# Another order of the first 100 steps of an attention and mixture-of-experts kernel on one Trainium2 core

## The chip, the core and the metric

The kernel runs as one program on one core of a Trainium2 chip. Five engines work side by side, each through its own queue in order: PE (TensorE, matrix products), DVE (VectorE), ACT (ScalarE), POOL (GpSimd) and SP (SyncE, which here issues nearly all transfers). Sixteen DMA engines move the data. The metric is the device time of one execution in microseconds (us); lower is better.

## The reference

Three parts follow each other. First, attention in which a query sees only the keys of its own bucket (a bucket is the sign pattern of six projections):

```python
q_bits = (np.einsum('bhsd,dk->bhsk', q, proj) > 0)
k_bits = (np.einsum('bhsd,dk->bhsk', k, proj) > 0)
mask = q_bucket[:, :, :, None] == k_bucket[:, :, None, :]
scores = np.where(mask, scale * np.matmul(q, k.transpose(0, 1, 3, 2)), -1e9)
attn = softmax(scores)
x = np.matmul(attn, v)
...
h = x @ w_in
x = (h * (1.0 / (1.0 + np.exp(-1.702 * h)))) @ w_out
...
logits = x @ w_gate + np.log1p(np.exp(x @ w_noise)) * noise
...
out[mask] += top2_w[mask, k, None] * (np.maximum(x[mask] @ w1[e], 0.0) @ w2[e])
```

Shapes: 2 batches, 8 heads, 768 positions, head width 64; so 1536 tokens of width 512. The feed-forward is 512 to 2048 to 512. The last part sends each token to 2 of 8 experts (512 to 1024 to 512). The weights `w_in` and `w_out` arrive as 64-bit numbers.

## The kernel before, in words

**Steps.** The attention is cut into 96 steps (`NU`), one for each batch, third of the positions, head and 128 queries. Six chunks of 16 steps make up the tokens: chunk 0 is steps 0 to 15, and so on. A loop over `g` emits for each step the scores of step g+2 (`qk`, line 250), the row maximum of step g+1 (`rowmax`, line 262, DVE), its exponential (`expo`, line 271, ACT), and the turning of the weights of step g. For steps 0 to 15 that turning is a transpose on PE (`e_turn`, line 289) and a copy out of PSUM (`e_copy`, line 297 or 299). From step 16 on it is a high half (`e_hi`, line 310, ACT), a low half (`e_lo`, lines 317 and 319) and a transposing DMA (line 323, `et<-er`). The buffers `er` of this last path are two, and they share their tag with the value blocks `v32` of the first chunk.

**Around it.** Everything else hangs on step numbers in a table `PARAM`. `KA` and `QA` say at which step a block of keys or queries is loaded (two steps ahead), split into halves (`stack_hi`, `stack_lo`), turned by DMA (line 169), projected (`buckets`, lines 186 and 187), compared (`one_hot`, line 197) and turned a second time with its bits (`stack_end`, line 205). `VA` does this for the values (lines 224, 225 and 232), `PV` for the products with the values (`pv`, lines 357 and 364) whose result is scaled and split into `xt` (`pv_scale` line 373, `pv_norm` line 380, `pv_out` lines 389 to 395). `ST` sets at which step a chunk's feed-forward begins, `RA` and `R1` when its routing runs, `O0` when the output is zeroed.

**Weight blocks.** The feed-forward weights come in 32 blocks of 512 KB: 0 to 15 of `w_in`, 16 to 31 of `w_out`. `W` gives each its step. A block is loaded (`w_load`, line 414, three buffers `wraw`), its 64-bit numbers are made 32-bit ones by three DVE operations (`w_bits`, lines 424, 427, 430), it is scaled (line 443 on POOL or 445 on ACT, by the table `WS`), its high half taken (line 446, ACT) and its low half (line 447, POOL). Only then is the buffer free for the block three later.

**Feed-forward.** `moe_pe` gives 16 pieces a chunk: eight of the first product (line 467, tiles `h`) and eight of the second (line 478, tiles `px`). Behind each `h` come a tanh (line 485, ACT), a product (line 497, DVE), a high half (line 511, ACT) and a low half (line 513, POOL or DVE by the table `GS`).

**What sets the order.** Up to step 99 the code only states in which order instructions are emitted; a scheduler then orders every engine's queue. From step 100 (`GM=100`) the order is the one written. So a number in the table does not fix a place; it changes what the scheduler sees, and the queues below show what came of it. On the chip each queue then runs strictly as it stands.

After the steps come the experts: products at lines 843, 868 and 874, each expert's weights split at lines 782 and 783, all in written order.

Of the kernel before, what the change touches and what calls it, by code (L numbers as in the profile page):

```python
# [57 lines left out]
PARAM = dict(GM=16, HE=lambda nm, b: 'D', OE=lambda nm, b: 'D', SC=lambda nm, b: 'D', WB=0, XO=lambda b: 'D', NG=16, WS=lambda i: 'P', TS=lambda g: True, XL=lambda g: 'D', GW=2, E0=7, T0=12, T1=16, EL=8, WX=3, PV={(1,2,3):4}, PVD=5, ST={}, VA={}, RA={}, O0=48, OS=2, IS=2, FU=16, VF=2, EC=lambda g: 'AA', QX=8, QS=3, EA=1, S1=(8,8,8,9,9,9,11,13), QE=8, XG=2, XB=2, PC=2, OH=3, BK=3, R0=18, R1=0, LK=8, WL=1, NW=3, LE=lambda nc: nc.scalar, I0=24, LQ=8, LV=0, W=[(g, 1) for g in range(-6, 30)], KA={(0,0,0):-8,(0,0,1):-6,(0,1,0):-4,(0,1,1):-2}, QA={(0,0,0):-7,(0,0,1):-3}, HI=lambda g: 'P', LO=lambda g: False)  # L58
PARAM.update(KA={(0, 0, 0): -15, (0, 0, 1): -6, (0, 1, 0): -5, (0, 1, 1): -4, (0, 2, 0): -1, (0, 2, 1): 1, (0, 3, 0): 4, (0, 3, 1): 5, (1, 0, 0): 37, (1, 0, 1): 39, (1, 1, 0): 44, (1, 1, 1): 46, (1, 2, 0): 42, (1, 2, 1): 51, (1, 3, 0): 47, (1, 3, 1): 51}, QA={(0, 0, 0): -15, (0, 0, 1): -3, (0, 0, 2): 1, (0, 0, 3): 3, (0, 1, 0): 8, (0, 1, 1): 9, (0, 1, 2): 17, (0, 1, 3): 21, (0, 2, 0): 24, (0, 2, 1): 28, (0, 2, 2): 30, (0, 2, 3): 33, (1, 0, 0): 37, (1, 0, 1): 41, (1, 0, 2): 47, (1, 0, 3): 52, (1, 1, 0): 57, (1, 1, 1): 56, (1, 1, 2): 60, (1, 1, 3): 69, (1, 2, 0): 72, (1, 2, 1): 69, (1, 2, 2): 80, (1, 2, 3): 84}, VA={(0, 0, 0): -1, (0, 0, 1): -3, (0, 1, 0): -1, (0, 1, 1): -1, (0, 2, 0): 0, (0, 2, 1): 0, (0, 3, 0): -1, (0, 3, 1): -2, (1, 0, 0): -1, (1, 0, 1): -1, (1, 1, 0): 2, (1, 1, 1): -4, (1, 2, 0): -3, (1, 2, 1): -3, (1, 3, 0): 2, (1, 3, 1): -2}, PV={(0, 0, 0): 4, (0, 0, 1): 5, (0, 0, 2): 6, (0, 0, 3): 5, (0, 1, 0): 6, (0, 1, 1): 4, (0, 1, 2): 4, (0, 1, 3): 5, (0, 2, 0): 5, (0, 2, 1): 5, (0, 2, 2): 5, (0, 2, 3): 6, (1, 0, 0): 4, (1, 0, 1): 5, (1, 0, 2): 4, (1, 0, 3): 5, (1, 1, 0): 5, (1, 1, 1): 5, (1, 1, 2): 5, (1, 1, 3): 6, (1, 2, 0): 6, (1, 2, 1): 4, (1, 2, 2): 4, (1, 2, 3): 4}, RA={0: 18, 1: 18, 2: 19, 3: 24, 4: 18}, W=[(g,1) for g in [-6, -4, -3, -1, 0, 0, 1, 1, 2, 4, 4, 7, 8, 8, 9, 10, 11, 12, 13, 14, 15, 16, 16, 17, 18, 20, 20, 22, 22, 23, 23, 24]], EC=lambda g:'AA', LE=lambda nc:nc.sync, HI=lambda g:'AAAA'[g%4], LO=lambda g:[0, 0, 0, 1, 0, 0, 0, 1][g%8]==1, S1=[8, 8, 8, 8, 8, 11, 13, 22], ST={0: 4, 1: 4, 2: 5, 3: 4, 4: 5, 5: 3}, NG=28, WS=lambda i:'PAAA'[i%4], HE=lambda nm,b:'DPDD'[2*(nm=='k')+b], OE=lambda nm,b:'DTDD'[2*(nm=='k')+b], SC=lambda nm,b:'DADD'[2*(nm=='k')+b], R1=2, I0=26, IS=1, O0=56, OS=1, GM=100, BK=3, OH=3, QX=7, QS=3, QE=8, VF=0, T0=12, T1=17, EL=10, WX=5, WL=2, PC=2, GW=2, E0=8, WB=2)

PARAM.update(H0=((15,1),(16,3)),H1=((0,5),(2,1)),HG=((1,1),),RT=0,E1=16,SL=1,QS=3)
# [1183 lines left out]
```

## Time and profile before

| what | value |
|---|---|
| time, median of 3 runs | 804.14 us (797.45 to 805.53) |
| the profiled execution's own time | 802.09 us |
| its span on the core | 800.3 us |
| what lies around the span | 1.8 us |
| PE busy | 705.8 us, 88% |
| DVE busy | 502.0 us, 63% |
| ACT busy | 457.7 us, 57% |
| POOL busy | 269.2 us, 34% |
| mean granted TensorE clock | 0.961 of full speed |

Busy shares are means over stages that have different limits. The steps run until about 450 us: row maximum 0 starts at 23.26 us, number 9 at 57.46, number 15 at 90.75, number 20 at 108.71, number 32 at 170.40, number 72 at 356.27 and number 95 at 450.66. The experts fill the last 250 us. The clock and the engines' shares are best read stage by stage between these marks.

### The profile page before, as it was taken

How to read it: one execution, taken by the hardware profiler on the slowest of the kernel's cores; microseconds unless marked ns; L12 is line 12 of the kernel's file. 1: busy time of each engine (PE TensorE's matmuls, PEld its weight loads, DVE VectorE, ACT ScalarE, POOL GpSimd, SP SyncE). 2: the span in 40 equal slices, each digit the busy share in tenths (PEclk: the TensorE clock that was granted, in tenths of full speed). 3: DMA queues.
4: the chain of work that ended last, by engine and by line, in shares of the span. 5: the costliest groups of instructions: out<-in, count | busy, mean ns of one | idle time of the engine just before them, and what ended most of it. 6: DMA issues, size and time to landing. Idle time of an engine off the chain costs nothing.

```text
span 800.3 us, 14889 instructions
## 1 busy us (share of the span) xinstructions
PE 705.8 (88%) x5408; PEld 434.1 (54%) x5409; DVE 502.0 (63%) x1251; ACT 457.7 (57%) x974; POOL 269.2 (34%) x338
## 2 busy tenths in 40 slices
PE   1776778988988889889989999998999999999995
PEld 0544446546744665467457667556555545555452
DVE  7986889887875788568667716672835427344220
ACT  4789877777776787467668514443543535435220
POOL 7445546552453355025122123241030211302113
PEclk9976889999989999999999999999999999999998
DMA  8999589999999999985696590658958568483213
GB/s 222 239 278 252 158 198 190 286 249 207 180 209 169 173 196 208 190 169 105 102 190 121 100 283 8 175 190 246 261 80 264 145 164 250 62 264 84 27 17 44
DMA packets 266941, 139.19 MB, mean 174 GB/s; under 512 B 224176, under 2 KB 242672, under 8 KB 266864
## 3 DMA queue, kind: packets, MB, share of 16 engines
q1 hardware_dynamic: 260848, 125.04, 67.3%
q0 software_dynamic: 6016, 13.16, 9.3%
q8 instruction: 43, 0.70, 0.4%
q14 instruction: 34, 0.28, 0.1%
HBM read 61.48 MB, written 23.20 MB: 106 GB/s over the span
## 4 chain that ended last, share of the span: by engine, by line
PE 39%; DMA 4%; DVE 3%; ACT 2%; issue 1%; POOL 1%; POOLq 0%; ACTq 0%; DVEq 0%
PE ph L843 15%; PE py L874 14%; PE px L478 5%; PE h L467 3%; DMA et<-er 3%; PE py L868 2%; PE pv L364 1%; DMA xg<-slots 1%; ACT er L310 1%; DMA slots<-xr,si 1%; PE s L250 0%; DVE er L319 0%; DVE th L497 0%; ACT ew L782 0%; POOL out_dram L891 0%
## 5 line engine op out<-in xcount | busy, mean ns | idle before, releaser
L467 PE MATMUL h<-xt,wi 128*128 128x256 f16 x1152 | 140.4, 278 | 11.6 <-ACT xt L393 5.6
L843 PE MATMUL ph<-xg,ew 128*128 128x400 f16 (+2 forms) x864 | 134.2, 317 | 3.6 <-DMA xg<-slots 2.9
L478 PE MATMUL px<-wo,gt 128*128 128x512 f16 x576 | 131.0, 380 | 0.4 <-DVE th L497 0.4
L467 PEld LDWEIGHTS <-wi 128*128 128x128 f16 x1152 | 113.1, 100 | 33.4 <-issue 13.4
L783 DVE SCALAR_TENSOR_TENSOR ew<-w,ew 128x1024 f16<-128x1024 f32 x64 | 77.8, 1226 | 82.3 <-ACT ew L782 82.3
L874 PE MATMUL py<-ew,ht 128*128 128x512 f16 x576 | 126.0, 379 | 0.0
L250 PE MATMUL s<-kt,qt 128*128 128x512 f16 (+3 forms) x384 | 89.9, 356 | 37.1 <-DVE e L262 26.2
L891 POOL DMA_INDIRECT out_dram<-yo,ti x32 | 49.9, 1558 | 207.2 <-ACT yo L884 196.4
L843 PEld LDWEIGHTS <-ew 128*128 128x128 f16 x864 | 81.9, 100 | 53.6 <-issue 5.6
L319 DVE SCALAR_TENSOR_TENSOR er<-e,mx,er 128x768 f16<-128x768 f32 x68 | 71.5, 1055 | 42.0 <-ACT er L310 40.8
L262 DVE TENSOR_SCALAR_CACHE_REDUCE e<-s 128x768 f32<-128x768 f32 x96 | 90.7, 949 | 4.4 <-PE s L250 1.4
L874 PEld LDWEIGHTS <-ht 128*128 128x128 f16 x576 | 56.3, 98 | 66.8 <-issue 0.2
L271 ACT ACTIVATE e<-e,mx 128x768 f32<-128x768 f32 x96 | 89.3, 930 | 1.7
L478 PEld LDWEIGHTS <-gt 128*128 128x128 f16 x576 | 55.0, 98 | 63.9 <-issue 2.0
L513 POOL TENSOR_TENSOR gt<-th,gt 128x512 f16<-128x512 f32 x48 | 56.5, 1176 | 97.8 <-ACT gt L511 94.7
L310 ACT ACTIVATE er<-e,mx 128x768 f16<-128x768 f32 x68 | 62.9, 930 | 33.2 <-DMA et<-er 31.1
L250 PEld LDWEIGHTS <-qt 76*128 76x128 f16 (+1 forms) x384 | 35.5, 102 | 67.4 <-issue 31.3
L884 ACT ACTIVATE yo<-py,wv 128x512 f32<-128x512 f32 x24 | 16.5, 687 | 93.4 <-PE py L874 56.7
L853 ACT ACTIVATE ht<-ph 128x400 f16<-128x400 f32 (+2 forms) x72 | 33.5, 465 | 57.5 <-PE ph L843 57.3
L782 ACT ACTIVATE ew<-w 128x1024 f16<-128x1024 f32 x64 | 66.2, 1048 | 0.1
L364 PE MATMUL pv<-et,vt 128*64 128x256 f16 x720 | 51.3, 285 | 11.4 <-DMA et<-er 11.3
L854 DVE SCALAR_TENSOR_TENSOR ht<-ph,ht 128x400 f16<-128x400 f32 (+2 forms) x72 | 37.4, 524 | 35.9 <-ACT ht L853 35.6
(230 smaller groups left out, 914.3 us busy)
## 6 DMA issues: line engine op xcount, KB each, us to landing
w<-in_moe_w_dram SPq DMA_DIRECT2D x64, 512.0 KB, 5.5
wraw<-in_moe_w_in_dram SPq DMA_DIRECT2D x16, 512.0 KB, 5.7
wraw<-in_moe_w_out_dram SPq DMA_DIRECT2D x16, 512.0 KB, 5.0
slots<-blank SPq DMA_DIRECT2D x6, 1032.0 KB, 7.4
v<-in_v_dram SPq DMA_DIRECT2D x24, 192.0 KB, 3.7
out_dram<-zeros SPq DMA_DIRECT2D x13, 256.0 KB
k<-in_k_dram SPq DMA_DIRECT2D x16, 192.0 KB, 4.0
q<-in_q_dram SPq DMA_DIRECT2D x24, 128.0 KB, 3.7
```

The source lines that it names most:

```text
L250: nc.tensor.matmul(ps[:, n0 * 128:n1 * 128], qt[:kr, s, h, t, :], kt[:kr, s, h, n0:n1, :].rearrange("p c t -> p (c t)"), start=(s == 0), s ...
L262: nc.vector.tensor_scalar(e32, st[g]["ps"][:, :S], -FAR, -TOP, op0=OP.max, op1=OP.max, accum_out=mx[:, 0:1])
L271: nc.scalar.activation(e32, e32, AF.Exp, scale=0.125, bias=st[g]["mx"][:, 1:2], accum_out=sms[b, cc, hp][:, 2 * h + t:2 * h + t + 1] if g ...
L310: nc.scalar.activation(er[:, 0], st[g]["e"], AF.Copy, scale=r)
L319: nc.vector.scalar_tensor_tensor(er[:, 1], d["e"], d["mx"][:, 3:4], er[:, 0], op0=OP.mult, op1=OP.subtract)
L364: nc.tensor.matmul(po[h * 64:h * 64 + 64, 0, :], vt[:, c, vs, h * 64:h * 64 + 64], et[h][:, es * NT + c].rearrange("p t q -> p (t q)"), st ...
L467: nc.tensor.matmul(ph[:, a, :], wi[ws][:, d, f0:f0 + 128], xt[:, d, xs, :], start=(d == 0 and ws == 0 and xs == 0), stop=(d == HP - 1 and ...
L478: nc.tensor.matmul(px, gts[ci, f // 2][:, gs, f % 2, t * 128:t * 128 + 128], wo[ws][:, f, :], start=(f == 0 and gs == 0 and ws == 0), stop ...
L782: nc.scalar.activation(hi, x, AF.Copy, scale=SW1 if j == 0 else SW2)
L783: nc.vector.scalar_tensor_tensor(lo, x, SW1 if j == 0 else SW2, hi, op0=OP.mult, op1=OP.subtract)
L843: nc.tensor.matmul(ph[:, :c1 - c0], w[:, ws, d * FE + f * 128:d * FE + f * 128 + 128], xg[e, p][:, xs * HP + d, :], start=(d == 0 and ws = ...
L874: nc.tensor.matmul(py, ht[:, f, hs, t * 128:t * 128 + 128], w[:, ws, f * DM:(f + 1) * DM], start=(i == 0), stop=(i == n - 1))
```

## The change

One line is added that replaces numbers and letters of the table; no function changes. All line numbers of the code below it grow by two.

```diff
+PARAM.update(KA={(0, 0, 0): -19, (0, 0, 1): -6, (0, 1, 0): -5, (0, 1, 1): -5,
...
+W=[(g_,1) for g_ in [-6, -4, -3, -1, 0, 0, 1, 1, 2, 3, 6, 6, 7, 8, 9, 10, 10, 10, 11, 12, 12, 12, 15, 15, 19, 20, 21, 23, 23, 26, 28, 29]],
...
+EC=lambda g:2*'AAAAAAADADAAAAAA'[g%16],
...
```

What differs, old value to new:

- Keys and queries: first key block from step -15 to -19, block (0,1,1) from -4 to -5, block (1,0,1) from 39 to 42, two later ones by one step. Query blocks (0,0,2) from 1 to -1, (0,0,3) from 3 to 1, (0,1,0) from 8 to 7, (0,1,3) from 21 to 19, two of batch 1 by one step.
- Values of head pair 0: `VA` -1 to 2 and -3 to -4.
- Value products `PV` (steps behind the unit's start): (0,0,0) 4 to 6, (0,0,1) 5 to 4, (0,0,2) 6 to 5, (0,1,2) 4 to 7, (1,2,2) 4 to 5.
- Weight blocks `W`: before `-6 -4 -3 -1 0 0 1 1 2 4 4 7 8 8 9 10 11 12 13 14 15 16 16 17 18 20 20 22 22 23 23 24`, now the list in the diff.
- `ST`: chunk 1's feed-forward from 4 to 6 steps behind its last attention step. `RA`: routing of chunk 2 from 19 to 22, of chunk 3 from 24 to 26; `R1` 2 to 0, so the last routing piece comes two steps sooner. `O0` 56 to 57.
- Engines: the two copies of line 297 in each of steps 7 and 9 from ACT to DVE; four low halves of line 513 (chunk 0 piece 7, chunk 1 piece 0, chunk 2 pieces 4 and 5) from POOL to DVE; the scaling of weight blocks 0, 12 and 24 from POOL to ACT; the high half of step 25 from ACT to POOL.

Three places show what the scheduler made of it.

The first is SP's queue between weight blocks 11 and 13 (blocks 11 and 12 are `wraw_677` and `wraw_717` before, `wraw_621` and `wraw_663` now; `v32` are value blocks). Before:

```order
L414 DMA wraw_677<-in_moe_w_in_dram 128x1024
L120 DMA q32_735<-in_q_dram 128x2x128
L120 DMA q32_778<-in_q_dram 128x2x128
L215 DMA v32_833<-in_v_dram 128x384 x2
L124 DMA v32_1107<-in_v_dram 128x384
L124 DMA v32_1196<-in_v_dram 128x384
L124 DMA v32_1290<-in_v_dram 128x384
L124 DMA v32_1292<-in_v_dram 128x384
L414 DMA wraw_717<-in_moe_w_in_dram 128x1024
```

Now:

```order
L416 DMA wraw_621<-in_moe_w_in_dram 128x1024
L207 DMA_TRANSPOSE qt_509<-qsb_458 128x4x128
L122 DMA q32_782<-in_q_dram 128x2x128
L416 DMA wraw_663<-in_moe_w_in_dram 128x1024
L171 DMA_TRANSPOSE qt_828<-qsa_787 128x4x128
L217 DMA v32_850<-in_v_dram 128x384 x2
L126 DMA v32_1014<-in_v_dram 128x384
L122 DMA q32_1185<-in_q_dram 128x2x128
L207 DMA_TRANSPOSE kt_659<-ks_638 128x6x128
L416 DMA wraw_694<-in_moe_w_in_dram 128x1024
```

Eight loads of queries and values stood between blocks 11 and 12; one load and a transpose stand there now, and the value loads are spread behind block 12.

The second is ACT's queue where the last quarter of chunk 0's `xt` is made, just before the first feed-forward (`er` are the high halves of steps 17 and 18, `xn` is `pv_scale`, `xt` is `pv_out`). Before:

```order
L310 ACTIVATE er_1186<-e32_1182 128x768
L310 ACTIVATE er_1218<-e32_1214 128x768
L373 ACTIVATE xn_1275<-pv_1232 128x256
L446 ACTIVATE wo0_92<-wraw_1063 128x512
L393 ACTIVATE xt_732<-xn_1275 128x256
```

Now:

```order
L312 ACTIVATE er_1210<-e32_1206 128x768
L375 ACTIVATE xn_1280<-pv_1239 128x256
L312 ACTIVATE er_1231<-e32_1227 128x768
L447 ACTIVATE wraw_953<-wraw_953 128x512
L395 ACTIVATE xt_853<-xn_1280 128x256
```

`xn` moved ahead of the second high half. The semaphores moved with it: before, the first `er` waits for a transposing DMA and the second for PE; now the first waits for PE, and the second, behind `xn`, for the DMA.

The third is ACT's queue where chunk 1's feed-forward begins (`th` are its first two tanh tiles, `er` the high halves of steps 35 and 36). Before:

```order
L310 ACTIVATE er_2221<-e32_2215,mx_2214 128x768
L158 ACTIVATE qsa_2275<-q32_2156 128x4x64
L310 ACTIVATE er_2294<-e32_2288,mx_2287 128x768
L485 ACTIVATE th_2411<-h_2379 128x512
L270 ACTIVATE mx_2321<-mx_2321 128x1
L485 ACTIVATE th_2531<-h_2427 128x512
```

Now:

```order
L312 ACTIVATE er_2219<-e32_2213,mx_2212 128x768
L487 ACTIVATE th_2525<-h_2491 128x512
L272 ACTIVATE mx_2321<-mx_2321 128x1
L487 ACTIVATE th_2605<-h_2540 128x512
L312 ACTIVATE er_2294<-e32_2288,mx_2287 128x768
```

The tanh tiles stand between the same exponentials as before, although the table puts the chunk two steps later, and they are now ahead of the second high half.

## Rows read from the trace of the kernel before

**Rows 1.** Page, part 1: busy time and share of each engine.
```profile
PE 705.8 (88%) x5408; PEld 434.1 (54%) x5409; DVE 502.0 (63%) x1251; ACT 457.7 (57%) x974; POOL 269.2 (34%) x338
```

**Rows 2.** Windows: length, then PE, PEld, DVE, ACT, POOL busy; PEclk, DMA share, GB/s.
```profile
23.26:57.46 34.20, 25.52 (x187) 16.47 (x184) 31.04 (x77) 27.47 (x75) 15.58 (x20) 0.87 1.14 259
57.46:92.56 35.10, 25.36 (x166) 15.11 (x165) 25.05 (x56) 30.42 (x80) 20.41 (x26) 0.69 0.91 241
...
108.71:170.40 61.69, 55.88 (x455) 36.84 (x454) 56.14 (x108) 46.49 (x99) 32.79 (x33) 0.93 0.97 229
170.40:356.27 185.87, 163.47 (x1405) 108.09 (x1403) 132.56 (x368) 130.33 (x307) 71.31 (x79) 0.96 1.01 194
...
543.00:800.30 257.30, 247.81 (x1681) 133.86 (x1680) 104.71 (x197) 98.14 (x145) 46.99 (x59) 0.99 0.58 146
```

**Rows 3.** Chain that ended last, in order of time: start, length, what.
```profile
402.72 5.80 DMA et<-er
...
430.26 2.12 PE pv L364 x35
```

**Rows 4.** Timeline at the start: us, length, engine, operation, [idle before <-releaser].
```profile
1.77 0.60 SPq L91 DMA_DIRECT2D p<-in_proj_dram  x1
...
23.26 0.94 DVE L262 TENSOR_SCALAR_CACHE_REDUCE e<-s 128x768 f32<-128x768 f32 x1
23.92 0.22 ACT L191 ACTIVATE pc<-s 128x72 f32<-128x72 f32 x1
```

**Rows 5.** Groups by line and shape: busy us, mean ns of one, idle before.
```profile
L424 DVE TENSOR_SCALAR pfi<-wraw 128x512 int32<-128x512 int32 x32 | 22.1, 690 | 11.7 <-DMA wraw<-in_moe_w_in_dram 10.7 <-DMA wraw<-in_moe_w_out_dram 0.8
L297 ACT ACTIVATE et<-pt 128x384 f32<-128x384 f32 x32 | 15.0, 482 | 1.1 <-PE pt L289 0.9
L380 DVE TENSOR_TENSOR xn<-pv,xn 128x256 f32<-128x256 f32 x7 | 2.9, 413 | 0.0
L513 POOL TENSOR_TENSOR gt<-th,gt 128x512 f16<-128x512 f32 x48 | 56.5, 1176 | 97.8 <-ACT gt L511 94.7 <-PE s L250 2.1 <-issue 0.9
L497 DVE SCALAR_TENSOR_TENSOR th<-th,h 128x512 f32<-128x512 f32 x48 | 32.6, 679 | 14.2 <-ACT th L485 9.6 <-issue 4.5
```

**Rows 6.** Timeline of DVE and POOL around 24 us.
```profile
23.05 0.28 DVE L197 TENSOR_TENSOR ks<-pc 128x36 f16<-128x36 f32 x2
...
23.95 1.15 POOL L447 TENSOR_TENSOR wi<-wraw,wi 128x512 f16<-128x512 f32 x1 [0.93 <-ACT wi L446]
24.17 1.10 DVE L197 TENSOR_TENSOR ks<-pc 128x36 f16<-128x36 f32 x2
```

**Rows 7.** Timelines of SP, DVE and POOL between 54 and 75 us.
```profile
54.17 2.04 SPq L124 DMA_DIRECT2D v<-in_v_dram  x4
57.10 0.33 SPq L414 DMA_DIRECT2D wraw<-in_moe_w_in_dram  x1
...
62.56 0.73 DVE L424 TENSOR_SCALAR pfi<-wraw 128x512 int32<-128x512 int32 x1 [1.99 <-DMA wraw<-in_moe_w_in_dram]
...
67.63 1.83 POOL L232 TENSOR_TENSOR vt<-v,vt 128x384 f16<-128x384 f32 x2
69.42 1.15 POOL L447 TENSOR_TENSOR wi<-wraw,wi 128x512 f16<-128x512 f32 x1
...
74.75 0.70 DVE L424 TENSOR_SCALAR pfi<-wraw 128x512 int32<-128x512 int32 x1 [4.66 <-DMA wraw<-in_moe_w_in_dram]
```

**Rows 8.** Timeline of ACT and PE where chunk 0's feed-forward starts.
```profile
103.69 1.58 ACT L310 ACTIVATE er<-e 128x768 f16<-128x768 f32 x2 [1.98 <-DMA et<-er]
105.18 0.36 ACT L373 ACTIVATE xn<-pv 128x256 f32<-128x256 f32 x1
107.36 0.42 ACT L393 ACTIVATE xt<-xn 128x256 f16<-128x256 f32 x1 [1.26 <-DVE xn L380]
107.83 0.58 PE L467 MATMUL h<-xt,wi 128*128 128x256 f16 x2 [5.61 <-ACT xt L393]
```

**Rows 9.** Waits: engine and line, waited for: total us, times, longest.
```profile
ACT er L310 <- DMA et<-er: 33.1, 23, 5.9
```

More of the change, by code (lines that the diff above doesn't have):

```diff
@@ L62 @@
 PARAM.update(XS=lambda nm,b:'P', GS=lambda ci,i:'P', XN='P', WS=lambda i:'paaa'[i%4])
+PARAM.update(KA={(0, 0, 0): -19, (0, 0, 1): -6, (0, 1, 0): -5, (0, 1, 1): -5, (0, 2, 0): -1, (0, 2, 1): 1, (0, 3, 0): 4, (0, 3, 1): 5, (1, 0, 0): 37, (1, 0, 1): 42, (1, 1, 0): 44, (1, 1, 1): 46, (1, 2, 0): 42, (1, 2, 1): 51, (1, 3, 0): 48, (1, 3, 1): 52},QA={(0, 0, 0): -15, (0, 0, 1): -3, (0, 0, 2): -1, (0, 0, 3): 1, (0, 1, 0): 7, (0, 1, 1): 9, (0, 1, 2): 17, (0, 1, 3): 19, (0, 2, 0): 24, (0, 2, 1): 28, (0, 2, 2): 30, (0, 2, 3): 33, (1, 0, 0): 37, (1, 0, 1): 41, (1, 0, 2): 47, (1, 0, 3): 52, (1, 1, 0): 57, (1, 1, 1): 56, (1, 1, 2): 60, (1, 1, 3): 69, (1, 2, 0): 73, (1, 2, 1): 68, (1, 2, 2): 80, (1, 2, 3): 84},VA={(0, 0, 0): 2, (0, 0, 1): -4, (0, 1, 0): -1, (0, 1, 1): -1, (0, 2, 0): 0, (0, 2, 1): 0, (0, 3, 0): -1, (0, 3, 1): -2, (1, 0, 0): -1, (1, 0, 1): -1, (1, 1, 0): 2, (1, 1, 1): -4, (1, 2, 0): -3, (1, 2, 1): -3, (1, 3, 0): 2, (1, 3, 1): -2},PV={(0, 0, 0): 6, (0, 0, 1): 4, (0, 0, 2): 5, (0, 0, 3): 5, (0, 1, 0): 6, (0, 1, 1): 4, (0, 1, 2): 7, (0, 1, 3): 5, (0, 2, 0): 5, (0, 2, 1): 5, (0, 2, 2): 5, (0, 2, 3): 6, (1, 0, 0): 4, (1, 0, 1): 5, (1, 0, 2): 4, (1, 0, 3): 5, (1, 1, 0): 5, (1, 1, 1): 5, (1, 1, 2): 5, (1, 1, 3): 6, (1, 2, 0): 6, (1, 2, 1): 4, (1, 2, 2): 5, (1, 2, 3): 4},RA={0: 18, 1: 18, 2: 22, 3: 26, 4: 18},ST={0: 4, 1: 6, 2: 5, 3: 4, 4: 5, 5: 3},W=[(g_,1) for g_ in [-6, -4, -3, -1, 0, 0, 1, 1, 2, 3, 6, 6, 7, 8, 9, 10, 10, 10, 11, 12, 12, 12, 15, 15, 19, 20, 21, 23, 23, 26, 28, 29]],O0=57,I0=26,GW=2,WL=2,BK=3,T0=12,T1=17,R1=0,VF=0,XS=lambda nm,b:'PPPPPP'[2*"qkv".index(nm)+b],SC=lambda nm,b:'DADD'[2*"qkv".index(nm)+b],HE=lambda nm,b:'DPDD'[2*"qkv".index(nm)+b],GS=lambda ci,i:'PPPPPPPDDPPPPPPPPPPPDDPPPPPPPPPPPPPPPPPPPPPPPPPP'[8*ci+i],XN='P',WS=lambda i:'aaaapaaapaaaaaaapaaapaaaaaaapaaa'[i],EC=lambda g:2*'AAAAAAADADAAAAAA'[g%16],HI=lambda g:'AAAAAAAAAAAAAAAAAAAAAAAAAPAAAAAAAAAAAAAAAAAAAAAAAAAAAAAAAAAAAAAAAAAAAAAAAAAAAAAAAAAAAAAAAAAAAAAA'[g],LO=lambda g:'DDDPDDDPDDDPDDDPDDDPDDDPDDDPDDPPPDPPPPDDPDPPPDPPPPPPPPPPPPPPPPPPPPPPPPPPPPPPPPPPPPPPPPPPPPPPPPPP'[g]=="P")
 @with_exitstack
```

## The prediction, made before the changed kernel ran

> **What bounds the kernel now.** I read the busy shares first: PE 88%, DVE 63%, ACT 57% [rows 1]. A mean like this hides that the program has several limits, so I cut it at row maxima and read the windows [rows 2]. In the last one, the experts, PE is busy for 247.81 of 257.30 us. Their order is the written one and the table does not reach it, so that stretch is worth nothing here. Everything must come from the time before it. Between 23 and 57 us DVE is the full engine, 31.04 of 34.20 us, and PE is not. Between 57 and 93 us it is ACT, 30.42 of 35.10, while DVE falls to 25.05. From 108.7 to 170.4 DVE has 56.14 and PE 55.88 of 61.69. From 170 to 356 PE has 163.47 of 185.87 us and the DMA engines are full (share 1.01). The chain that ended last runs through a transposing DMA of 5.80 us at 402.72 and enters PE's unbroken work at 430.26 [rows 3]. So the early stretch has idle engines to win, the middle is tight on PE and transfers together, and the end is fixed. What is gained before 170 us reaches the end only if the middle carries it through.
>
> The sum is made against the profiled execution's own 802.09 us (a span of 800.3 and 1.8 around it). That is 2.05 us under the median of 804.14.
>
> **Start, 0 to 23 us.** SP now issues the two loads of the projection before the first query load. Each holds SP for 0.60 us [rows 4], so queries come 1.2 us later. The first row maximum now also stands behind the comparisons of the third and fourth key block, whose copy out of PSUM begins at 23.92 and takes 0.22 [rows 4]. It cannot start before about 24.4, where it started at 23.26. The second maximum then follows at once, so part of this comes back. The first key block's step of -19 changes nothing: its load was the first in SP's queue already. Bounds 0 and +1.5; I take **+0.5**.
>
> **Steps 1 to 9, 23 to 57 us.** Between row maxima 0 and 9 DVE's queue held 22 weight operations and now holds 25. Three more at 0.69 us [rows 5] are 2.1. Two of the PSUM copies of steps 7 and 9 come onto DVE here. No DVE copy of that size is in the trace: the DVE operation on 256 columns from PSUM takes 0.41 [rows 5], the maximum over 768 takes 0.94 [rows 4]; for 384 I take 0.5, near the lower row and near the 0.48 that ACT needs [rows 5]. Together +3.1 on the engine that is full. Its idle time in this stretch is 3.2 us [rows 2], and it may serve for part of this if blocks arrive in time. Bounds +1 and +3; I take **+1.8**.
>
> A second price lies in this stretch. Two comparisons that took 0.28 us at 23.05 took 1.10 at 24.17, when a POOL subtraction had been running since 23.95 [rows 6]. The Trainium skill (SBUF — State Buffer, "Who interferes with whom") says that the port pair which DVE shares with POOL is locked by one of them for a whole instruction; the trace agrees. By that rule the low half of the one extra weight block would hold DVE up by some 0.8 us more (1.10 less 0.28), and the sum below would end 0.8 us higher.
>
> **Steps 9 to 15, 57 to 93 us.** Here the new order is strongest. DVE, in order, waits 1.99 us for weight block 12 at 62.56 and 4.66 us for block 14 at 74.75, with the next row maxima queued behind [rows 7]. Block 12 was issued at 57.10, after eight loads of queries and values, four of which alone held SP for 2.04 us from 54.17 [rows 7]. Now one load and one transpose stand between blocks 11 and 12. Block 14 had to wait for the buffer of block 11, whose low half POOL did at 69.42, behind value halves that began at 67.63 [rows 7]; in the new POOL queue that low half stands ahead of all value halves. So both causes, 6.65 us, are touched. But ACT is next: its 30.42 us of work [rows 2] grow by about 1.0 (four value operations and one scaling come in from before, three copies go out, each near the 0.48 of the copies [rows 5]). The stretch cannot fall under about 31.4 us; from 35.1 I let it reach 31.8. Bounds -3.7 and 0; I take **-3.3**.
>
> **Chunk 0's feed-forward starts, 93 to 108 us.** PE stood 5.61 us, until 107.83, for the last quarter of `xt` [rows 8]. The products for it were long done. Its scaling `xn` ran on ACT only at 105.18, because two high halves stood ahead, the first of which waited 1.98 us for a transposing DMA, until 103.69; `xt` came at 107.36 [rows 8]. Now one high half without that wait stands ahead of `xn`, and only the second, behind it, waits for the DMA. That one still stands ahead of `xt`: it ends at about 103.69 + 0.8 = 104.5, the scaling of a weight block adds 0.7, so `xt` can start at 105.1. That is 2.3 us sooner. Its DVE product has its place ahead of the second low half and is ready by then. Bounds -5.6 (PE's whole wait) and 0 (the row maximum behind is late for another reason); I take **-2.3**.
>
> **Chunk 1's feed-forward.** The title's two steps are not what the queues show: its first tanh tiles stand between the same exponentials as before, but ahead of the second high half. Those high halves wait for the transposing DMA 23 times, 33.1 us in all, 1.4 each [rows 9]. One high half of 0.8 and one such wait, 2.2 us, is the most that goes; PE has scores and value products to do meanwhile. Bounds -2.2 and 0; I take **-1.0**.
>
> **Edits that I cost at nothing.** Four low halves go from POOL to DVE: 1.18 us there [rows 5], between 0.41 and 0.94 here, and 0.68 by the nearest two-input row of that size [rows 5]. They stand at steps 27 to 58; three of the four lie where DVE has 53 us idle in 186 [rows 2], the first costs 0.7 where it has 5.5. Three scalings from POOL to ACT: the one inside the full ACT stretch is in the sum above. One high half from ACT to POOL at step 25: POOL has 32.79 busy of 61.69 [rows 2]; if POOL is late with it, the low half on DVE and the transposing DMA behind it wait up to 1 us. Routing, scatter and zero-filling only change places among themselves: nothing waits for them before the experts, and if the fills meet a weight block, that is the last rival. Between 108 and 356 us the counted DVE work to row maximum 32 is the same before and now, 54 us from maximum 20, and the feed-forward runs up to 9 us of PE work further ahead of the scores in between, then is level again by step 72. I take 0, with +4 and -9 as bounds.
>
> **The sum.** 0.5 + 1.8 - 3.3 - 2.3 - 1.0 = -4.3, so 802.1 - 4.3 = **797.8 us**, 0.8% under the median. One per cent, 8 us, is about what a measurement of this kernel can tell from no change.
>
> **Rivals.**
>
> *The middle hands it back.* Transfers are full from 108 to 356 us (0.97 and 1.01 [rows 2]). If they are the true limit there, an early start only makes queries and weights queue behind transposes. For it: the chain goes through a transposing DMA [rows 3]. Against it: the share is also busy time stretched by others, and after 356 us steps are still paced by PE. The queues that hardly moved for chunk 1 fit it too: the change then does less than it says. Time: 802.
>
> *The middle gains as well.* Between 108.7 and 356.3 us PE is idle for 28.2 us, and its granted clock is 0.93 and 0.96 [rows 2]. The mean is 0.952, so about 23.6 of the 247.6 us ran at the lower of the two levels (1.2 instead of 2.4 GHz), and up to half of that, 11.8 us, can come back. With the feed-forward further ahead PE has work where it stood. A fifth of the idle time (5.6) and 0.4 of the clock (4.7) give 10 us. For it: the low clock (0.69 from 57 to 93) comes with idle PE. Against it: the same total work and the same transfers. Time: 788.
>
> *The last weights come too late: slower.* The last three blocks moved from steps 23, 23, 24 to 26, 28, 29, and the pieces of `px` that need them stand at step 31. In SP's queue three blocks (0.52 MB each) now follow two zero-fills of 1.06 MB; 3.7 MB at 229 GB/s [rows 2] are 16 us. If PE reaches those pieces before that, it stops in order, with the scores behind it, and every later step is that much later. It decides as soon as DVE's operations on block 29 come after PE's last ready `px` product. Against it: before, three fills stood ahead of these blocks, and DVE's last weight operation now comes two row maxima sooner (behind number 30 instead of 32). Time: 797.8 + 16 = 814.
>
> **How the numbers follow.** The forecast 0.48, with its own range of 793 to 803 (the terms' bounds, not all at one end); the middle hands it back 0.17; the middle gains 0.22; late weights 0.13. Of the forecast's 0.48, 0.18 lies below 796.1, which is 1% under the median. Faster by over 1%: 0.18 + 0.22 = 0.40. Within 1%: 0.30 + 0.17 = 0.47. Slower: 0.13. The range of 785 to 808 leaves out the late weights and the far end of the gain.
>
> **What would show it.** Right: the two waits of DVE for weight blocks near 62 and 75 us gone or under 2 us together; row maximum 9 one to three us later than 57.46, maximum 15 level with or before 90.75; PE's wait before chunk 0's feed-forward near 3 us instead of 5.61; row maximum 72 about 4 us before 356.27; the experts as long as before, 257 us. Wrong: maximum 72 no earlier than before (the middle handed it back), or 10 us and more earlier with a clock nearer to full (it gained as well), or PE standing at line 478 behind the low halves of the last blocks (late weights).

## The result and the profile after

The changed kernel took 806.15 us (median of 21 runs, 802.26 to 809.40); the kernel before, in 21 runs with it, 800.36 us (796.92 to 805.59). The ratio is 1.0059 with a 95% interval of 1.0043 to 1.0075. The change made the kernel about 0.6%, or some 5 us, slower. The forecast, 797.8 us, had the other sign. It was compared with 804.14 us, a median of three runs; against the 800.36 us of 21 runs it stands for a gain of 0.3%, not 0.8%. The profiled execution after took 809.40 us, the longest of its 21, and has a span of 807.7 us, 7.4 more than the one before. So the two profiles lie further apart than the medians do (5.8 us), and differences of two or three microseconds between them can be chance.

The busy shares say nothing of it. Page after, part 1:

```profile
PE 707.3 (88%) x5408; PEld 433.8 (54%) x5409; DVE 510.3 (63%) x1259; ACT 456.6 (57%) x972; POOL 263.2 (33%) x332
```

The windows after, between the same row maxima as [rows 2] (with the columns given there):

```profile
27.00:68.85 41.85, 27.47 (x195) 17.46 (x195) 34.67 (x80) 29.05 (x78) 16.16 (x21) 0.75 1.05 227
68.85:101.13 32.28, 23.63 (x146) 14.20 (x144) 25.11 (x52) 27.07 (x72) 18.09 (x22) 0.74 0.79 224
...
118.45:177.82 59.37, 53.85 (x451) 34.89 (x450) 56.39 (x110) 46.64 (x100) 34.28 (x35) 0.99 1.00 232
177.82:365.25 187.43, 164.66 (x1420) 108.45 (x1419) 133.26 (x366) 129.91 (x307) 65.22 (x72) 0.95 1.00 190
550.00:807.70 257.70, 247.63 (x1681) 133.71 (x1680) 104.42 (x197) 98.13 (x145) 47.44 (x61) 0.98 0.62 146
```

Read the lengths against [rows 2]. Row maximum 0 starts at 27.00 instead of 23.26 (+3.7). From number 0 to 9 it takes 41.85 us instead of 34.20 (+7.7). From 9 to 16 it is 32.28 instead of 35.10 (-2.8), and the experts are unchanged. The loss is made in the first 69 us, on the engine that was full there. Between maxima 0 and 9 DVE's work grew by 3.6 us (31.04 to 34.67), and its idle time by 4.0 (3.2 to 7.2).

The chain that ended last enters PE's long run of work behind a transposing DMA, near the place of [rows 3]:

```profile
415.71 5.46 DMA et<-er
...
423.84 1.87 PE h L469 x8
```

**The start.** Timeline after of SP, PE, DVE and POOL up to row maximum 0 (compare [rows 4] and [rows 6]):

```profile
1.31 0.60 SPq L93 DMA_DIRECT2D p<-in_proj_dram  x1
...
23.26 0.82 PE L252 MATMUL s<-kt,qt 76*128 76x512 f16 x2 [5.89 <-DMA qt<-qsb]
...
24.45 0.28 DVE L145 TENSOR_SCALAR qsb<-q 128x256 f16<-128x256 f32 x1
24.68 0.30 DVE L199 TENSOR_TENSOR ks<-pc 128x36 f16<-128x36 f32 x2
24.95 0.94 DVE L153 TENSOR_SCALAR qsa<-qsb 128x256 f16<-128x256 f16 x1
25.91 1.16 DVE L199 TENSOR_TENSOR ks<-pc 128x36 f16<-128x36 f32 x2
27.00 0.94 DVE L264 TENSOR_SCALAR_CACHE_REDUCE e<-s 128x768 f32<-128x768 f32 x1
```

The scores of step 0 are complete at 24.08 (23.26 + 0.82). Their maximum runs at 27.00, because the split and scaling of a later query block and four comparisons stand ahead of it in DVE's queue.

**Steps 3 to 4.** Timeline after of PE, then of DVE, between row maxima 3 and 4:

```profile
38.04 0.49 PE L252 MATMUL s<-kt,qt 76*128 76x512 f16 x2
...
38.67 0.48 PE L252 MATMUL s<-kt,qt 76*128 76x512 f16 x2
...
45.91 0.76 PE L350 MATMUL pv<-ident,r 128*64 128x128 f16 x8 [5.35 <-DVE r L340]
46.47 5.33 PE L359 MATMUL pv<-et,v 128*64 128x256 f32 x24
```

```profile
38.64 0.59 DVE L153 TENSOR_SCALAR qsa<-qsb 128x256 f16<-128x256 f16 x1
41.62 0.69 DVE L426 TENSOR_SCALAR pfi<-wraw 128x512 int32<-128x512 int32 x1 [2.39 <-DMA wraw<-in_moe_w_in_dram]
...
44.69 1.17 DVE L340 CAST r<-sm 128x4 f16<-128x4 f32 x1
...
46.34 0.95 DVE L264 TENSOR_SCALAR_CACHE_REDUCE e<-s 128x768 f32<-128x768 f32 x1
```

This is the centre of the loss. The scores of steps 4 and 5 are complete at 38.53 and 39.15. DVE stands idle from 39.23 to 41.62 for weight block 7, with the ready maximum 4 queued behind; it runs at 46.34, 7.8 us after its scores. Before, scores 4 were complete at 36.51 and their maximum ran at 37.33:

```profile
35.67 0.84 PE L250 MATMUL s<-kt,qt 76*128 76x512 f16 x2
...
37.33 0.95 DVE L262 TENSOR_SCALAR_CACHE_REDUCE e<-s 128x768 f32<-128x768 f32 x1
```

In the changed kernel PE has no matmul from 40.6 to 45.9, since the factor `r` for the next value products is made behind the same weight. The windows of this stretch show what follows:

```profile
40.60:45.90 5.30, 0.00 (x0) 0.00 (x0) 4.04 (x10) 2.64 (x8) 2.03 (x2) 0.58 1.01 243
45.90:51.72 5.82, 5.81 (x32) 2.99 (x33) 5.35 (x15) 3.26 (x8) 2.75 (x3) 0.51 1.12 223
```

When PE starts again, its granted clock is 0.51, close to the lower of its two levels, and 24 value products take 5.33 us. The same 24 before, at a granted clock of 1.00:

```profile
40.81 2.76 PE L357 MATMUL pv<-et,v 128*64 128x256 f32 x24
```

**Steps 9 to 16.** DVE's timeline after, against [rows 7]:

```profile
67.80 0.68 DVE L426 TENSOR_SCALAR pfi<-wraw 128x512 int32<-128x512 int32 x1
...
77.76 0.68 DVE L426 TENSOR_SCALAR pfi<-wraw 128x512 int32<-128x512 int32 x1
...
84.50 0.69 DVE L426 TENSOR_SCALAR pfi<-wraw 128x512 int32<-128x512 int32 x1 [3.70 <-DMA wraw<-in_moe_w_in_dram]
```

Blocks 12 and 14 are no longer waited for (1.99 and 4.66 us before). Block 15 now is, 3.70 us, just ahead of row maximum 12, and block 17, 1.32 us, at 94.25. All waits for weight blocks in this stretch fell from 7.4 to 5.4 us.

**The first feed-forward.** Timeline after of ACT and PE, against [rows 8]:

```profile
112.67 0.36 ACT L375 ACTIVATE xn<-pv 128x256 f32<-128x256 f32 x1
113.80 0.84 ACT L312 ACTIVATE er<-e 128x768 f16<-128x768 f32 x1 [0.77 <-DMA et<-er]
...
115.08 0.40 ACT L395 ACTIVATE xt<-xn 128x256 f16<-128x256 f32 x1
...
115.54 0.38 PE L469 MATMUL h<-xt,wi 128*128 128x256 f16 x2 [3.99 <-ACT xt L395]
```

PE's wait fell from 5.61 to 3.99 us. This product starts 7.7 us later than before (107.83), so in this pair of profiles the lateness is +8.6 at maximum 16, +7.7 here and +7.4 at the end. In between it is not steady: +9.0 at maximum 72 and +3.2 at maximum 95. The waits view after, against [rows 9]:

```profile
ACT er L312 <- DMA et<-er: 36.1, 25, 2.7
```

### The profile page after: what moved, and what is told of

It is laid out like the page before. It is cut to its first block, busy times and chain, and to the rows that moved or that the text cites. A ratio compares the mean times of both kernels' runs of the same rounds, so it can differ in the third digit from the quotient of the medians.

```text
span 807.7 us, 14886 instructions
## 1 busy us (share of the span) xinstructions
PE 707.3 (88%) x5408; PEld 433.8 (54%) x5409; DVE 510.3 (63%) x1259; ACT 456.6 (57%) x972; POOL 263.2 (33%) x332
## 3 DMA queue, kind: packets, MB, share of 16 engines
q1 hardware_dynamic: 260848, 125.04, 68.9%
## 4 chain that ended last, share of the span: by engine, by line
PE 46%; DMA 8%; DVE 6%; ACT 5%; issue 2%; POOL 1%; SPq 0%; POOLq 0%; ACTq 0%; DVEq 0%
PE ph L845 15%; PE py L876 13%; PE px L480 9%; DMA et<-er 6%; PE h L469 4%; PE py L870 2%; PE pv L366 1%; PE s L252 1%; ACT er L312 1%; DMA qt<-qsb 1%; ACT e L273 1%; DVE er L321 1%; DVE e L264 1%; DMA xg<-slots 1%; ACT gt L513 1%
## 5 line engine op out<-in xcount | busy, mean ns | idle before, releaser
L480 PE MATMUL px<-wo,gt 128*128 128x512 f16 x576 | 134.8, 387 | 3.6 <-POOL gt L515 1.9
L252 PE MATMUL s<-kt,qt 128*128 128x512 f16 (+3 forms) x384 | 87.2, 349 | 31.2 <-DVE e L264 21.8
L515 POOL TENSOR_TENSOR gt<-th,gt 128x512 f16<-128x512 f32 x44 | 54.0, 1226 | 93.0 <-ACT gt L513 92.0
L856 DVE SCALAR_TENSOR_TENSOR ht<-ph,ht 128x400 f16<-128x400 f32 (+2 forms) x72 | 37.3, 523 | 35.9 <-ACT ht L855 35.6
```

Of the source, the lines that this page charges most:

```text
L252: nc.tensor.matmul(ps[:, n0 * 128:n1 * 128], qt[:kr, s, h, t, :], kt[:kr, s, h, n0:n1, :].rearrange("p c t -> p (c t)"), start=(s == 0), s ...
L480: nc.tensor.matmul(px, gts[ci, f // 2][:, gs, f % 2, t * 128:t * 128 + 128], wo[ws][:, f, :], start=(f == 0 and gs == 0 and ws == 0), stop ...
```

## The experiments

The theory after this reading: the new key and query steps put splits, comparisons and a weight wait ahead of row maxima that are ready, and DVE works its queue in order. The rivals: the new engine letters or weight steps are the loss; or the end is set after 108 us and the head does not count. "Letters" are the changed entries of `EC`, `WS`, `GS` and `HI`.

All runs, with the start of four row maxima (one profile each, us) and the ratio to the kernel before that ran beside it:

| run | max 0 | max 4 | max 9 | max 20 | ratio, 95% interval |
|---|---|---|---|---|---|
| before | 23.3 | 37.3 | 57.5 | 108.7 | 1 |
| changed | 27.0 | 46.3 | 68.9 | 118.5 | 1.0059 [1.0043, 1.0075] |
| e1 key and query steps undone | 24.4 | 38.2 | 60.3 | 108.5 | 1.0025 [1.0003, 1.0047] |
| e2 key and query steps alone | 26.9 | 47.1 | 68.3 | 121.2 | 1.0179 [1.0146, 1.0211] |
| e3 letters undone | 26.6 | 46.0 | 66.7 | 119.8 | 1.0133 [1.0099, 1.0167] |
| e4 weight steps undone | 26.9 | 46.5 | 68.5 | 117.4 | 1.0083 [1.0058, 1.0109] |
| e5 letters alone | 24.4 | 38.5 | 60.9 | 109.7 | 0.9956 [0.9923, 0.9990] |
| e6 weight steps alone | 24.1 | 37.9 | 58.0 | 108.9 | 1.0004 [0.9979, 1.0029] |
| e7 value steps alone | 24.2 | 38.5 | 57.7 | 110.5 | 1.0012 [0.9987, 1.0037] |
| e8 feed-forward, routing alone | 24.5 | 38.7 | 59.5 | 111.1 | 0.9993 [0.9969, 1.0018] |
| e9 changed, tie at max 5 | 26.8 | 42.9 | 65.3 | 112.9 | 1.0040 [1.0016, 1.0064] |
| e10 letters, tie at max 7 | 24.3 | 38.1 | 59.2 | 107.9 | 0.9987 [0.9962, 1.0012] |
| e11 key block (0,1,1) alone | 28.0 | 44.6 | 66.9 | 118.6 | 1.0159 [1.0116, 1.0202] |
| e12 two query blocks alone | 23.9 | 48.4 | 69.0 | 117.6 | 1.0202 [1.0165, 1.0238] |
| e13 changed, two ties | 27.4 | 45.8 | 70.8 | 116.1 | 1.0057 [1.0039, 1.0075] |
| e14 key, query steps and letters | 27.0 | 46.7 | 67.8 | 118.9 | 1.0051 [1.0025, 1.0077] |
| e15 first key block alone | 25.2 | 39.4 | 59.1 | 111.3 | 0.9988 [0.9966, 1.0010] |
| e16 letters, feed-forward steps | 23.8 | 36.9 | 60.2 | 108.0 | 0.9965 [0.9944, 0.9987] |
| e17 before, max 4 behind block 7 | 23.8 | 41.8 | 62.0 | 114.5 | 1.0001 [0.9978, 1.0024] |
| e18 before, max 4 behind block 8 | 24.9 | 47.8 | 68.9 | 120.8 | 1.0098 [1.0070, 1.0126] |

Kernels whose queues are those of before up to maximum 9 (e6, e7, e8 and, but for a few exchanges in the first 18 us, e15) have that maximum at 57.7 to 59.5, so a head read from one profile is good to about 2 us.

Two things limit what the runs can say. In e6 every engine's trace has the same instructions in the same order as before, to the end: the weight steps alone change nothing, and e6 is a second sample of the kernel before (its span is 797.2 us, 3.1 shorter). In the other runs the scheduler rearranges the queues of all engines from some point on, also behind the place that the edit is aimed at. The exception is e15.

### Which edits: undone

e1, e3 and e4 give one group of numbers its old values in the changed kernel (in this order; only what changes is shown):

```diff
-KA: (0, 0, 0): -19, (0, 1, 1): -5, (1, 0, 1): 42, (1, 3, 0): 48, (1, 3, 1): 52
+KA: (0, 0, 0): -15, (0, 1, 1): -4, (1, 0, 1): 39, (1, 3, 0): 47, (1, 3, 1): 51
-QA: (0, 0, 2): -1, (0, 0, 3): 1, (0, 1, 0): 7, (0, 1, 3): 19, (1, 2, 0): 73, (1, 2, 1): 68
+QA: (0, 0, 2): 1, (0, 0, 3): 3, (0, 1, 0): 8, (0, 1, 3): 21, (1, 2, 0): 72, (1, 2, 1): 69
```

```diff
+PARAM.update(EC=lambda g:'AA', WS=lambda i:'paaa'[i%4], GS=lambda ci,i:'P', HI=lambda g:'A')
```

```diff
+PARAM.update(W=[(g,1) for g in [-6, -4, -3, -1, 0, 0, 1, 1, 2, 4, 4, 7, 8, 8, 9, 10,
+    11, 12, 13, 14, 15, 16, 16, 17, 18, 20, 20, 22, 22, 23, 23, 24]])
```

> The changed kernel with the key and query steps (KA, QA) of before; all else as changed. Theory 'early order': the new key and query steps alone put comparisons, splits and a wait for weight block 7 ahead of row maxima 0, 4 and 8; the chunk 0 attention is 8 to 10 us late by row maximum 9 and the steady stretch carries 5 to 7 of it to the end. Then row maximum 0 is back at 23 to 24 us, number 4 near 38 (46.3 changed), number 9 near 58 to 60 (68.9 changed), and the time is 5 us or more below the changed kernel: ratio to before 0.99 to 1.00. Rival 'middle': the end is set by transfers and PE after 108 us and an early gain is handed back; then row maximum 9 is early all the same but the time stays at 1.004 to 1.008 of before. Rival 'weights and engines': maxima 4 and 9 stay late (46 and 68).

> The changed kernel with the engine letters of before (copies of steps 7 and 9, scaling of three weight blocks, four low halves, one high half back on their old engines). Theory 'early order': the first 9 row maxima stay late (number 4 near 46, number 9 at 66 to 68, its two copies on DVE gone), time within 0.3% of the changed kernel: 1.003 to 1.009 of before. Rival 'engines': the letters are the loss; row maximum 9 near 58 to 60, time at or under before.

> The changed kernel with the weight steps (W) of before. Theory 'early order': nothing changes ahead of row maximum 20 (the queues are the same there), time within 0.3% of the changed kernel: 1.003 to 1.009 of before. Rival 'late weights': the later steps of the last five blocks delay the second products of chunk 0; then row maxima 24 and 28, which run 13 us late in the changed kernel (9.7 at number 20), come back by some 3 us and the time falls to 1.000 to 1.003 of before.

Measured: with the old key and query steps the head is back (maximum 9 at 60.3) and the time falls to 1.0025. That is 0.34% below the changed kernel, less than the 5 us expected. Undoing the letters made it worse, by 0.74%, outside what was expected: they are a gain, not the loss. Undoing the weight steps left the time within the uncertainty of the changed kernel.

### Which edits: alone

The same groups the other way round, new values in the kernel before: e2 has the first diff reversed, e5 the second, e6 the third, e14 the first two. e7, then e8, then e15 are below (what is not named stays); e16 is e5 and e8 together.

```diff
+VA: (0, 0, 0): 2, (0, 0, 1): -4
+PV: (0, 0, 0): 6, (0, 0, 1): 4, (0, 0, 2): 5, (0, 1, 2): 7, (1, 2, 2): 5
```

```diff
+ST: 1: 6
+RA: 2: 22, 3: 26
+R1=0, O0=57
```

```diff
+KA: (0, 0, 0): -19
```

> The kernel before with the new key and query steps alone. Theory 'early order': row maximum 4 near 46 and number 9 near 66 to 69 us, time 1.005 to 1.012 of before, since the gain between maxima 9 and 15 comes from it only in part. Rival 'middle': maxima late but the time within 0.3% of before. Rival 'weights and engines': maxima as before (37 and 57), time as before.

> The kernel before with the new engine letters alone (copies of steps 7 and 9 on DVE, scaling of three weight blocks on ACT, four low halves on DVE, one high half on POOL). In the changed kernel undoing them cost 5.5 us. Theory 'letters gain by themselves' (POOL and ACT are relieved between row maxima 9 and 20): 0.993 to 0.998 of before, row maximum 15 at 87 to 89 us instead of 90.75, number 9 up to 2 us later. Rival 'letters only help a late head': within 0.2% of before.

> The kernel before with the new weight steps alone. The queues are those of before up to row maximum 17. Theory 'weight steps are nearly free': within 0.3% of before. Rival 'late weights': the last blocks delay the second products of chunk 0; 1.004 or more of before, with PE waiting at the second product for a weight block's half.

> The kernel before with the new steps of the value blocks and of the value products (VA, PV) alone. Theory 'the loss is the head': within 0.3% of before, row maxima 0 to 17 as before. Rival 'value products come too late' (the product of chunk 0, head pair 0 two steps later, of chunk 1, head pair 2 three steps later): row maxima 18 to 40 over 2 us later and 1.004 or more of before.

> The kernel before with chunk 1's feed-forward two steps later, the routing of chunks 2 and 3 later, the last routing piece sooner and the zeroing at 57 (ST, RA, R1, O0) alone. Theory 'the loss is the head': within 0.3% of before up to 0.3% faster. Rival 'feed-forward too late': PE runs short of work between row maxima 32 and 56, 1.004 or more of before.

> The kernel before with the new key and query steps and the engine letters; weight, value, feed-forward and routing steps as before. Theory 'the letters are the repair': 1.005 to 1.010 of before, and with it the changed kernel's time. Rival 'the value, weight and feed-forward steps repair a late head too': 1.010 to 1.016.

> The kernel before with the first key block's step at -19 instead of -15, nothing else. DVE's queue is that of before from row maximum 0 on; in SP's queue the two projection loads go ahead of the first query load. Theory 'only DVE's order costs': row maximum 0 at 23.3 to 25, number 9 at 57 to 60, time within 0.3% of before. Rival 'the late query load is the start's loss': row maximum 0 at 25.5 or later and 1.003 or more.

> The kernel before with the engine letters (0.9956 alone) and the new feed-forward and routing steps (0.9993 alone). If both add: 0.993 to 0.997 of before. Rival 'they do not add' (undoing the key and query steps left letters, weight, value and feed-forward steps at 1.0025): 0.999 or more.

Measured: the key and query steps alone cost 1.79%, more than the theory said. The letters alone gain 0.44%, and this version beats both kernels; but maximum 15 runs at 91.8 us in it, not at 87 to 89, so the gain lies elsewhere than expected. Value and feed-forward steps are within 0.12% of before. So are the weight steps, but as they change no queue here, e6 does not test them. Key and query steps with the letters give 1.0051, the changed kernel's time: so its 0.59% is the loss of the one, partly repaired by the other. The first key block's step does nothing measurable. The later feed-forward adds nothing to the letters. The parts do not add up in every combination: e1, which is the letters with the weight, value and feed-forward steps, is 0.7% above the letters alone, though none of these steps costs anything alone. Which of them spoils it was not run.

### Which key or query step

e11, then e12, take one edit each into the kernel before:

```diff
-KA: (0, 1, 1): -4
+KA: (0, 1, 1): -5
```

```diff
-QA: (0, 0, 2): 1, (0, 0, 3): 3
+QA: (0, 0, 2): -1, (0, 0, 3): 1
```

> The kernel before with key block (0,1,1) one step sooner, nothing else. Its comparisons and the transpose behind them go ahead of row maximum 0; between maxima 3 and 4 stand 9 operations (8 before, 18 in the changed kernel), with block 7 among them. Theory 'ready maxima wait in DVE's queue': row maximum 0 at 25.5 to 27 (23.3 to 24.5 before), number 4 at 38 to 42, number 9 at 59 to 65, time 1.000 to 1.008 of before. Rival 'the query steps are the loss, the key step is harmless': row maximum 9 below 60, time within 0.2% of before.

> The kernel before with query blocks (0,0,2) and (0,0,3) two steps sooner, nothing else. 25 operations with blocks 7 and 8 stand between row maxima 3 and 4 in DVE's queue (8 before, 18 in the changed kernel). Theory 'ready maxima wait in DVE's queue': row maximum 4 at 50 to 56 us, number 9 at 63 to 70, time 1.008 to 1.020 of before. Rival 'the start (projection and comparisons ahead of maximum 0) is the loss': row maximum 0 as before (23.3 to 24.5), number 4 late, but number 9 below 61 and time within 0.3% of before.

Measured: either edit alone spoils the head as much as all together (maximum 9 at 66.9 and 69.0, all together 68.3). They do it at different places: e11 has maximum 0 late, at 28.0, and e12 has it as before but takes 16 us from maximum 3 to 4, with a wait of 2.78 us for block 7. Their times, 1.0159 and 1.0202, lie above the ends expected, 1.008 and 1.020; for e11 every maximum is later than said too, and in e12 maximum 4, at 48.4, is earlier than said. What makes maximum 4 late in e11 is only in part the order of DVE's queue. PE's scores 4 wait there for a transposing DMA and are complete at 42.05 (36.51 before):

```profile
41.23 0.82 PE L252 MATMUL s<-kt,qt 76*128 76x512 f16 x2 [2.90 <-DMA qt<-qsb]
```

### DVE's order, with no step moved

e17 moves no step of the kernel before; it ties row maximum 4 behind weight block 7 in DVE's queue. e18 has `last[8]` in its place. The scheduler answers the tie on the other engines too: the queues of PE, ACT and POOL differ from before from 38 to 43 us on, that of SP from 44 (e17) or 48 (e18).

```diff
+        if g == 4:
+            tc.add_manual_dep(m.ins, last[7].ins.name, mybir.DependencyInfo(
+                mybir.DependencyClass.NoSync, mybir.DependencyReason.DATA))
```

> The kernel before, all its steps, with row maximum 4 tied behind the third operation of weight block 7 in DVE's queue (15 operations between maxima 3 and 4 instead of 8). Theory 'ready maxima wait in DVE's queue': row maximum 4 at 42 to 45 us (37 to 39 before), number 9 at 60 to 64, time 1.002 to 1.010 of before. Rival 'the loss comes from the moved keys and queries themselves (their loads, transposes and buffers), DVE's order only shows it': number 9 below 60 and time within 0.2% of before.

> The same with row maximum 4 behind block 8 (22 operations). Theory 'ready maxima wait in DVE's queue': a larger dose of the same, row maximum 4 at 47 to 51, number 9 at 64 to 70, time 1.008 to 1.020 of before. Rival as in e17: number 9 below 60 and time within 0.2% of before.

Timeline of PE in e18 behind these ties:

```profile
39.92 2.88 PE L362 MATMUL pv<-et,v 128*64 128x256 f32 x24
...
48.82 1.46 PE L250 MATMUL s<-kt,qt 128*128 128x512 f16 x4 [6.02 <-DVE e L264]
```

Measured: e18 has the changed kernel's head (maximum 4 at 47.8, number 9 at 68.9), and costs 0.98%, with no key or query step moved. PE waits 6.02 us for the maximum. So a maximum queued behind weight blocks is enough for this head, and a loss of about this size needs no moved step. That DVE's order alone causes the loss is not shown, since the other queues changed as well. In the profiles of e2, e11, e12 and e18 the lateness does not come back: 9 to 12 us at maximum 9, 8 to 16 at maxima 20, 32, 40, 56, 72 and 95, 12 to 15 at the end. The smaller dose, e17, has maximum 4 at 41.8 and maximum 9 at 62.0, close to what was expected, but its median is that of before: 1.0001, where 1.002 or more was expected. Its profile does not show how: that execution took 808.48 us, the longest of its 12, and was late to the end (4.5 us at maximum 9, 6.5 at the end).

### Mending the changed kernel

e9 ties block 7's first operation, head pair 2's comparisons, one key split and the gate operation behind row maxima 4 and 5 and behind the making of the first `r`. e13 also ties head pair 1's key comparisons behind maxima 0 and 1. e10 is the same kind of tie on the kernel with the letters, for blocks 8 and 9 at maxima 6 and 7. The core of e9:

```diff
+            if i in (7,):
+                held.append(w)
...
+        if g in (4, 5):
+            behind(m)
```

> The changed kernel with all its steps, but block 7's first weight operation, the comparisons of head pair 2's keys and queries, one key split and the gate operation are tied behind row maximum 5 in DVE's queue. 15 operations and no weight wait stand between row maxima 3 and 4, where 18 with a wait of 2.39 us stood. Theory 'ready maxima wait in DVE's queue' (scores 4 were ready at 39.2 us, their maximum ran at 46.3): row maximum 4 at 39 to 42, number 9 at 60 to 65 instead of 68.9, time 0.998 to 1.003 of before, so 2 to 6 us below the changed kernel. Rival 'DVE is simply full; what is taken ahead of maximum 4 comes back behind it': maximum 4 early, number 9 within 1.5 us of 68.9, time as the changed kernel (1.004 to 1.008).

> The changed kernel with the tie of e9 and a second one: the comparisons of head pair 1's two key blocks stand behind row maxima 0 and 1 in DVE's queue. Theory 'ready maxima wait in DVE's queue': row maximum 0 at 24 to 25.5 (27.0 changed, 23.3 to 24.5 before), number 4 at 40 to 43, number 9 at 61 to 64, time 0.998 to 1.004 of before. Rival 'the early lateness is not what the end pays for': number 9 as said but the time at 1.004 to 1.008.

> The kernel before with the new engine letters (0.9956 alone) and, by the same tie, weight blocks 8 and 9 and the gate operation behind row maximum 7 in DVE's queue: before, scores 6 were ready at 40.6 us and their maximum ran at 49.27, behind 19 operations and a weight wait of 1.45. Theory 'ready maxima wait in DVE's queue': row maximum 6 at 44 to 47, number 9 at 54 to 58 (60.9 with the letters alone), time 0.988 to 0.996 of before. Rival 'DVE is full': number 9 within 1.5 us of 60.9 or the weights come late, time 0.996 to 1.003.

DVE's timeline in e9:

```profile
41.01 0.36 DVE L152 TENSOR_SCALAR ks<-k 128x384 f16<-128x384 f32 x1 [1.27 <-DMA k<-in_k_dram]
...
42.86 0.95 DVE L275 TENSOR_SCALAR_CACHE_REDUCE e<-s 128x768 f32<-128x768 f32 x1
```

And in e13:

```profile
26.75 0.73 DVE L165 TENSOR_SCALAR qsa<-qsb 128x256 f16<-128x256 f16 x1 [1.51 <-ACT qsa L172]
27.40 0.95 DVE L276 TENSOR_SCALAR_CACHE_REDUCE e<-s 128x768 f32<-128x768 f32 x1
...
40.14 0.43 DVE L157 TENSOR_SCALAR qsb<-q 128x256 f16<-128x256 f32 x1 [2.60 <-DMA qt<-qsb]
```

Measured: e9 brings maximum 4 forward by 3.5 us and number 9 by 3.6, a little less than expected, since key splits that wait for their loads now stand ahead of it. Its time, 1.0040, lies below that of the changed kernel, but the intervals overlap; it is above the range of the theory and in that of the rival. (The 39.2 us of the expectation is when the scores of step 5 were complete; those of step 4 were at 38.53.) e13 failed as a mend. With the comparisons gone from ahead of maximum 0, the scaling of a query block stands there and waits 1.51 us for ACT; the next query split waits 2.60 us for a transposing DMA. The head stays at least as late as in the changed kernel, and so does the time (1.0057). That is the time of its rival, but as the head did not move, e13 decides nothing. e10 has maximum 6 at 47.8 instead of 50.4 and number 9 at 59.2 instead of 60.9, and gains nothing: 0.9987, where the letters alone gave 0.9956. Both maxima are later than the theory said, and the time is in the range of the rival. So of the tests by ties only e18 met the theory in its time. A shift of the head by a few microseconds (e9, e10, e17) could not be found again in the time.

## Why the prediction was wrong, step by step

**What bounds the kernel: right in place, wrong in use.** DVE was read as the full engine from 23 to 57 us. That full stretch is where the change loses.

**Start, +0.5: mis-sized, +3.7.** It was said that the first maximum "cannot start before about 24.4". Counted were the copy ahead of the comparisons (to 24.14) and, by the numbers, one pair of them undisturbed (0.28). The 1.2 us by which queries were to come later are not in it. The scores themselves came 1.75 us later (21.51 to 23.26); the split and scaling of a query, 0.28 and 0.94 us, stood ahead as well; and the second pair of comparisons took 1.16. That price stood in [rows 6] and was left out of the sum. The first key block's step cost nothing measurable, as said (e15).

**Steps 1 to 9, +1.8: the step that failed, +7.7.** The added work was right: 3.1 us estimated, and the three weight operations and two copies take 3.1 in the trace; the other 0.5 of the 3.6 are small operations that took longer. What failed is the sentence that DVE's idle time of 3.2 us "may serve for part of this if blocks arrive in time". The idle time did not serve: it rose to 7.2 us, since in an ordered queue an early operation brings its wait with it: 2.39 us for block 7, 1.60 at 63.45 for the load of a query block, 0.91 for block 11. I counted how many weight operations stood between maxima 0 and 9, but not between which two of them, nor whether the scores behind were ready. Between maxima 3 and 4 stand 9 operations in DVE's queue before and 19 in the changed kernel, block 7's three among them (the expectations of the runs miscount such rows by one or two).

**Steps 9 to 15, -3.3: near, in part by luck.** Measured -2.8 over the window from which the term was worked out (35.10 to 32.28). Both waits went, as said. But ACT did not become the floor: its work was to grow to 31.4 us and fell to 27.07, with part of it done ahead of the window. What stopped the gain at nearly the same place were new waits of DVE, 3.70 us for block 15 above all.

**Chunk 0's feed-forward, -2.3: right in kind, smaller.** PE's wait fell by 1.6 us. `xn` does go ahead of the second high half, but an exponential and a weight's high half now end just before it. From maximum 16 to PE's product it is 14.41 us instead of 15.27, which is -0.9, within the scatter of single profiles.

**Chunk 1's feed-forward, -1.0, and the rest, 0.** From PE's product to the end it is 692.2 us, 692.5 before: the rest 0 came out, but as a balance. The key and query steps lose and the letters gain (next paragraph), and the execution profiled after took longer than its kernel's median. Of the -1.0 nothing is to be seen. ACT's waits for the transposing DMA did not shrink (36.1 us, 33.1 before).

**The letters, costed at nothing or as a small loss: wrong sign.** They gain 0.44% alone (e5), and 0.7 to 1.3% beside the late head (e3 against the changed kernel, e2 against e14). Some 2 us of that are there by maximum 20 (121.2 and 119.8 in e2 and e3, 117.4 to 118.9 in the changed kernel, e4 and e14, which have the same queues up to about 155 us). Where they save the rest is not settled: behind that single profiles scatter by several microseconds. So the forecast had an error of each sign, and the 0.6% is what the two leave.

The measured pieces, 3.7 + 7.7 - 2.8 - 0.9 - 0.3 = 7.4 us, cut the difference of the two spans at marks in time, so they must add up to it; the sum does not say what caused each piece.

**The rivals.** The sign "maximum 72 no earlier than before" came true, but not for the reason of its rival: the middle had no early start to hand back, and it passed a late head on. The slower rival was the wrong place. The second products waited 3.6 us in all, 1.9 of it for a low half of POOL and 1.7 for the high halves of two weight blocks, where 16 were feared, and giving the weight blocks their old steps did not help (e4). The page after, part 5:

```profile
L480 PE MATMUL px<-wo,gt 128*128 128x512 f16 x576 | 134.8, 387 | 3.6 <-POOL gt L515 1.9
```

What happened was on no list: a ready maximum behind a weight that was not there yet.

**What stays open.** e18 and e2 have the same head, but cost 0.98% and 1.79%, and e17 is 4.5 us late at maximum 9 and costs nothing. So how much of a late head the end pays is not settled. What e2, e11 and e12 lose beyond e18 lies behind maximum 9, where their queues differ from each other on every engine; no run says what it is.

## What to carry to other kernels

When a step is moved forward, list what comes to stand ahead of each ready result on the full engine, and ask of every one of them when its own data lands: the wait of the first that is late is paid by all that stand behind it. Idle time of a full engine is cover only for work whose inputs are already there. A table that changes many things at once should be split into its parts: here one part loses 1.8% alone, one gains 0.4%, and the others do nothing by themselves. And where a scheduler stands between the table and the queues, compare the queues first: one of the parts had changed none, and a tie meant for one engine changed all.
